# Second mixture, first expert: the next expert's weights prepared nine steps sooner, and the Sinkhorn rounds in rising order

## The chip, the core and the metric

The kernel runs on one core of a Trainium2 chip. The metric is device time in microseconds of one execution; lower is better. The core has TensorE (PE: matmuls and transposes, into PSUM), VectorE (DVE), ScalarE (ACT), GpSimd (POOL) and SyncE (SP, whose queue issues most loads). Each engine works off its own instructions strictly in their order and waits on semaphores for the others.

## The reference

Three stages in one program: attention with queries averaged in pairs, a first mixture that dispatches each token to one expert, and a second mixture in which all 8 experts work on all 1152 tokens. Only the second is touched. Its inputs are x (1152 x 512), w1 (8 x 512 x 1024) and w2 (8 x 1024 x 512):

```python
logits = x @ w_gate
logits = logits - logits.max()
P = np.exp(logits)
for _ in range(8):
    P /= P.sum(1, keepdims=True) + 1e-09
    P /= P.sum(0, keepdims=True) + 1e-09
    P *= N / E
for e in range(E):
    h = np.maximum(x @ w1[e], 0.0)
    ye = h @ w2[e]
    out += P[:, e:e + 1] * ye
```

## The kernel before

Every fp32 operand is split into a pair of fp16 matrices, a high and a low part, scaled by a power of two that comes from its largest magnitude. For a weight matrix that takes: four size reductions on DVE, one per quarter (`amx`, tile `wmx`); a transpose on PE that brings the 128 lanes together (`fa`, tile `wmt`); a small matmul that spreads the result (`fb`, tile `wmp`); a few instructions of DVE to the scale; then high parts on ACT (L159) and low parts on DVE (L164).

In the second mixture the first expert (`e == 0`, weights number 8) runs a plain first layer: 24 steps of 12 matmuls, over three chunks of 256, 384 and 512 columns of tokens with 8 steps each (tile `g`; ACT writes `hh`, DVE writes `hl`). Then the second layer: 9 tiles of tokens with 24 matmuls each (L1550 to L1552), each folded into `acc` by DVE. From the second expert on, layer 1 is one level of Winograd's form (L1373), so its w1 needs four sums on POOL (`w1_sums`, L1341 and L1344) between its parts `o1` to `o7`, and x needs sums too: `x_sums`, eight sums on POOL for each half of the tokens with splits on ACT and DVE, done once, while the first expert runs.

The order of all this beside the matmuls is written out by hand in slots. `at(sl, k, f)` puts a piece of work into slot k, `run(sl, k)` emits it behind step k. For the first expert slots 0 to 23 are the steps of layer 1, and slots 24 to 41 (NL is 24) are two for each tile of layer 2: one in its middle, one at its end. `PM` holds the slots of the weights' work, `XS` those of the rest. The raw w1 and then the raw w2 of the next expert use one buffer (`r`), so the load of w2 waits until all of w1 has been worked off, and the load of the following w1 until all of w2 has been.

The gate's eight Sinkhorn rounds stand in layer 1 as well. A round is `sk_col` (a column sum by a matmul, tile `pc`, L1262, and four instructions of DVE) and `sk_row` (four of DVE). The eighth is `sk_end` in place of a row step: it writes the gate `Pf`, from which `fac` and so `acc` follow. `XS[20]` to `XS[27]` are the slots of the eight rounds; before, the last two are 23 and 22.

Of the kernel before, what the change touches and what calls it, by code (L numbers as in the profile page):

```python
# [42 lines left out]
AHX_ENG = ['dve', 'dve', 'dve', 'act', 'act', 'any', 'act', 'any', 'dve']  # L43
LAG = 6
LOD = 1
PM = [21, 22, 22, 24, 26, 27, 27, 33, 0, 8, 4, 4, 4, 6, 7, 9, 10, 10, 13, 13, 9, 13, 16, 15, 18, 20, 0, 6, 13]
BGP = 100
XM = "ddddddppp"
# [2 lines left out]
LT = 3  # L51
LE = 4
XTA = [1, 3, 5, 7]
XS = [0, 1, 1, 2, 5, 5, 6, 7, 0, 0, 3, 3, 5, 6, 7, 8, 9, 9.5, 10, 11, 12, 13.5, 15, 16, 18, 20, 23, 22]
LG = [3, 2, 2, 2]
PT = {6: 'act'}
A_SCALE = 2.0 ** A_BITS
# [4 lines left out]
def attn_moe_sinkhorn(ctx, tc, q, k, v, wg1, wa1, wa2, wg2, wb1, wb2, out, cap):  # L62
# [21 lines left out]
    wZ = ctx.enter_context(tc.tile_pool(name="wZ", bufs=1))  # L84
    drp = ctx.enter_context(tc.tile_pool(name="drp", bufs=1, space=DRAM))

# [1 line left out]
    idf = cst.tile([P, P], F32, name="idf")  # L88
    make_identity(nc, idf)
    idh = cst.tile([P, P], F16, name="idh")  # L90
# [26 lines left out]
        nc.sync.dma_start(wg1f, wg1.rearrange("(c p) e -> p c e", p=P))  # L117
        nc.sync.dma_start(wg2f, wg2.rearrange("(c p) e -> p c e", p=P))

# [1 line left out]
    def pow2(pool, m, n, T, tag):  # L121
        b = pool.tile([P, n], I32, tag=tag + "b", name=tag + "b")
        s = pool.tile([P, n], I32, tag=tag + "s", name=tag + "s")
# [39 lines left out]
    def lo(o, i, s, h):  # L163
        nc.vector.scalar_tensor_tensor(out=o, in0=i, scalar=s, in1=h, op0=ALU.mult, op1=ALU.subtract)  # L164

# [1 line left out]
    wraw = {}  # L167
    wset = {}
    WN = ("1h", "1l", "2h", "2l", "s")
# [98 lines left out]
    xd = drp.tile([N, 2 * DM], F16, name="xd")  # L268
    yd = drp.tile([E * cap, DM], F32, name="yd")

    # ================= attention =================
    rt = ctx.enter_context(tc.tile_pool(name="rt", bufs=1))
    lgs = rt.tile([P, NT, E], F32, name="lgs")
    mrow = rt.tile([P, NT], F32, name="mrow")
# [624 lines left out]
            if t >= ji:  # L899
                tl_av(t)  # L900

    # ================= routing =================
    actx.close()
    wpools[0, 1] = ctx.enter_context(tc.tile_pool(name="wB2", bufs=1))
    m1 = ExitStack()
# [77 lines left out]
    fac1 = rt.tile([P, NT], F32, name="fac1")  # L983
    tt(fac1, gate, isx, ALU.mult)

    # ================= first mixture: dispatched experts =================
    gp = m1.enter_context(tc.tile_pool(name="gp", bufs=2))
    xTs = {}
    wgh = rt.tile([P, KD, E], F16, name="wgh")
# [21 lines left out]
    def at(slots, k, f):  # L1011
        slots.setdefault(k, []).append(f)
# [34 lines left out]
                    at(slots, base + l[j][c], lambda j=j, c=c: lo_(j, c))  # L1047

    def keep_warm(n):
        # the array's clock halves after a few idle microseconds  # L1050
        pw = ps_i.tile([P, 512], F32, tag="mi", name="warm")
        for _ in range(n):
            nc.tensor.matmul(pw[:, :cap], lhsT=idh, rhs=iocap, start=True, stop=True)
# [100 lines left out]
    keep_warm(80)  # L1154
    sg, ig = yq["g"]

    # ================= combine =================
    m1.close()
    m2 = ctx.enter_context(tc.tile_pool(name="m2", bufs=1))
    m2s = ctx.enter_context(tc.tile_pool(name="m2s", bufs=2))  # L1160
# [74 lines left out]
            out=lg2[:, t, :], in0=pl[:, :E], scalar1=isx2[:, t : t + 1], scalar2=None, op0=ALU.mult  # L1235
        )

    # ================= Sinkhorn gate, run beside the first expert =================
    Pm = m2.tile([P, NT, E], F32, name="Pm")
    Pf = m2.tile([P, NT, E], F32, name="Pf")  # L1240
    rs = m2.tile([P, NT], F32, name="rs")
# [32 lines left out]
        nc.vector.tensor_scalar(out=rs, in0=isx2, scalar1=sg, scalar2=None, op0=ALU.mult)  # L1274
        tt(Pf, Pm, bc(rs), ALU.mult)

    # ================= second mixture: every expert on every token =================
    # From its second expert on, the first layer is one level of Winograd's form of
    # Strassen's product, on halves of w1's columns, of the model width and of the tokens.
    wx = []  # L1280

    def wino_open():
# [176 lines left out]
    for e in range(E):  # L1459
        i = E + e  # L1460
        sl = {}
        for k_, fs_ in carry.items():
            for f_ in fs_:
                at(sl, k_, f_)
        carry = {}
        if e == 0:
            for t in range(2):
                c_max(t)
            c_scale(0, 2)
            for f_ in (c_hi, c_lo, c_tr):  # L1470
                for t in (1, 0):
                    f_(t)
            for t in range(2, 5):
                c_max(t)
            c_scale(2, 5)
            for t in range(2, 5):
                at(sl, XS[t - 2], lambda t=t: (c_hi(t), c_lo(t)))
                at(sl, XS[t - 2] + 1, lambda t=t: c_tr(t))
            for t in range(5, NT):
                at(sl, XS[3], lambda t=t: c_max(t))  # L1480
            at(sl, XS[3], lambda: c_scale(5, NT))
            for t in range(5, NT):
                at(sl, XS[t - 1], lambda t=t: (c_hi(t), c_lo(t)))
                at(sl, XS[t - 1] + 1, lambda t=t: c_tr(t))
            for t in range(NT):
                at(sl, XS[8 + t], lambda t=t: c_lg(t))
            at(sl, XS[17], lambda: red(nmx, lg2.rearrange("p t e -> p (t e)"), ALU.max))
            at(sl, XS[18], sk_a)
            at(sl, XS[19], sk_b)
            at(sl, XS[19], sk_row)  # L1490
            at(sl, XS[19], wino_open)
            for k_ in range(8):
                at(sl, XS[20 + k_], sk_col)
                at(sl, XS[20 + k_], sk_row if k_ < 7 else sk_end)
            w1_plan(sl, i + 1, PM[:4], PM[4:6], PM[6])
            for s_ in range(2):
                xs_ = x_sums(s_)
                for j in range(9):
                    at(sl, NL + PM[8 + s_] + j, lambda xs_=xs_: next(xs_))
            b_ = PM[7]  # L1500
        elif e + 1 < E:
            w1_plan(sl, i + 1, PM[20:24], PM[24:26], NL + PM[26])
            b_ = NL + PM[27]
        if e + 1 < E:
            at(sl, b_, lambda i=i: w_load(i + 1, 1))
            amx, fa, fb, hi_, lo_ = [lambda *a_, i=i, m=m: preps[i + 1][m](*a_) for m in range(5)]
            w2q = [lambda c=c, amx=amx: amx(1, c) for c in range(4)]
            w2q += [lambda fa=fa: fa(1), lambda fb=fb: fb(1)]
            w2q += [lambda c=c, hi_=hi_, lo_=lo_: (hi_(1, c), lo_(1, c)) for c in range(4)]
            nxt = {}  # L1510
            if e + 2 < E:
                w2q.append(lambda i=i: w_load(i + 2, 0))
            for g_, k_ in zip(w2q, PM[10:20] + [PM[28]]):
                if b_ + k_ < NL + 18:
                    at(sl, b_ + k_, g_)
                else:
                    nxt.setdefault(b_ + k_ - NL - 18, []).append(g_)
        if e == 0:
            w1h, w1l = [wset[i][n_] for n_ in WN[:2]]
            for ch in range(3):  # L1520
                cs_ = slice(XG[ch] * P, (XG + [NT])[ch + 1] * P)
                QC = cs_.stop - cs_.start
                for f in range(KF):
                    fs = slice(f * P, (f + 1) * P)
                    ps = ps_g.tile([P, 512], F32, tag="g", name="g3")
                    for c in range(KD):
                        nc.tensor.matmul(ps[:, :QC], lhsT=w1h[:, c, fs], rhs=xT2[:, c, cs_], start=(c == 0), stop=False)
                        nc.tensor.matmul(
                            ps[:, :QC], lhsT=w1h[:, c, fs], rhs=xT2[:, KD + c, cs_], start=False, stop=False
                        )  # L1530
                    run(sl, ch * KF + f - 0.5)
                    for c in range(KD):
                        nc.tensor.matmul(
                            ps[:, :QC], lhsT=w1l[:, c, fs], rhs=xT2[:, c, cs_], start=False, stop=(c == KD - 1)
                        )
                    nc.scalar.activation(hh[:, f, cs_], ps[:, :QC], AF.Relu)
                    nc.vector.scalar_tensor_tensor(
                        out=hl[:, f, cs_], in0=ps[:, :QC], scalar=0.0, in1=hh[:, f, cs_], op0=ALU.max, op1=ALU.subtract
                    )
                    run(sl, ch * KF + f)  # L1540
        else:
            rest = wino_l1(i, sl)
        w2h, w2l, i12 = [wset[i][n_] for n_ in WN[2:]]
        fac = m2s.tile([P, NT], F32, tag="fac", name=f"fac{e}")
        nc.vector.tensor_scalar(out=fac, in0=Pf[:, :, e], scalar1=i12, scalar2=None, op0=ALU.mult)
        for k_, t in enumerate((0, 1, 5, 2, 3, 4, 6, 7, 8) if e else range(NT)):
            ts_ = slice(t * P, (t + 1) * P)
            ps = ps_g.tile([P, 512], F32, tag="g", name="g4")
            for f in range(KF):
                nc.tensor.matmul(ps[:, :DM], lhsT=hh[:, f, ts_], rhs=w2h[:, f], start=(f == 0), stop=False)  # L1550
                nc.tensor.matmul(ps[:, :DM], lhsT=hh[:, f, ts_], rhs=w2l[:, f], start=False, stop=False)  # L1551
                nc.tensor.matmul(ps[:, :DM], lhsT=hl[:, f, ts_], rhs=w2h[:, f], start=False, stop=(f == KF - 1))  # L1552
                if f == 3 and (k_ or not e):
                    run(sl, NL + 2 * k_)
            if e and not k_:
                rest()
                run(sl, NL)
            if e == 0:
                nc.vector.tensor_scalar(
                    out=acc[:, t, :], in0=ps[:, :DM], scalar1=fac[:, t : t + 1], scalar2=None, op0=ALU.mult  # L1560
                )
            else:
                nc.vector.scalar_tensor_tensor(  # L1563
                    out=acc[:, t, :], in0=ps[:, :DM], scalar=fac[:, t : t + 1], in1=acc[:, t, :],
                    op0=ALU.mult, op1=ALU.add,
                )
            if e == E - 1:
                nc.sync.dma_start(out[t * P : (t + 1) * P, :], acc[:, t, :])
            run(sl, NL + 2 * k_ + 1)
        assert not sl, sorted(sl)  # L1570
        carry = nxt if e + 1 < E else {}
# [29 lines left out]
```

## Time and profile before

| what | value |
|---|---|
| device time, median of 3 runs | 1335.86 us (1335.6 to 1338.24) |
| span of the profiled execution | 1332.0 us |
| PE busy | 1211.0 us, 91% |
| DVE busy | 985.2 us, 74% |
| ACT busy | 610.5 us, 46% |
| POOL busy | 362.4 us, 27% |

The page gives no device time of its own for the profiled execution; its span runs from the first to the last instruction, 3.9 us less than the median. Busy time of PE counts slow matmuls as busy, so the granted clock has to be read beside it. The second mixture fills about the last 770 us of the span; its first expert runs from 566.6 to 690.7 us.

### The profile page before, as it was taken

To read this page: it belongs to the slowest core of one execution; us is meant where nothing else is said; L and a number is where in the kernel's file an instruction comes from. 1 tells how busy PE (TensorE), PEld (TensorE's weight loads), DVE (VectorE), ACT (ScalarE), POOL (GpSimd) and SP (SyncE) were. 2 spreads that over 40 slices of the span, in tenths; PEclk is the share of its full clock that TensorE was granted. 3 is DMA by queue.
4 is the path that set the end of the run, shared out by engine and by line. 5 is a ranking of instruction groups with operands and counts; after the bars stand their busy time and mean duration, and the time that the engine had idled before them with its cause. 6 is when DMAs were issued, how large, how long until landed. Compare 5 with 4: busy or idle time off the path is not lost.

```text
span 1332.0 us, 21634 instructions
## 1 busy us (share of the span) xinstructions
PE 1211.0 (91%) x8796; PEld 771.6 (58%) x8796; DVE 985.2 (74%) x1752; ACT 610.5 (46%) x974; POOL 362.4 (27%) x193
## 2 busy tenths in 40 slices
PE   5786879786999999799879999999999999999998
PEld 2444545454777777674346466466475574664763
DVE  5989989997776768467869668677587595686741
ACT  5777767764778876341223323234133133232320
POOL 2665757672124321202631100101011011001000
PEclk9878888886999999999989999999999999999999
DMA  7999999994797784200011110110110211101001
GB/s 219 210 209 227 210 209 206 195 178 128 243 287 237 232 226 162 86 5 1 1 63 64 59 69 1 64 64 1 63 64 1 80 48 62 66 1 63 1 20 53
DMA packets 232996, 145.82 MB, mean 109 GB/s; under 512 B 188672, under 2 KB 197888, under 8 KB 232896
## 3 DMA queue, kind: packets, MB, share of 16 engines
q1 hardware_dynamic: 228560, 133.16, 40.0%
q0 software_dynamic: 2256, 7.08, 1.7%
q10 hardware_dynamic: 2080, 4.19, 0.9%
q8 instruction: 69, 1.13, 0.3%
q14 instruction: 31, 0.25, 0.1%
HBM read 88.38 MB, written 9.44 MB: 73 GB/s over the span
## 4 chain that ended last, share of the span: by engine, by line
PE 58%; DVE 22%; DMA 7%; ACT 6%; issue 4%; POOL 1%; SPq 1%; another core or an unknown queue 0%; POOLq 0%; ACTq 0%; DVEq 0%
PE g L1550 7%; PE g L1552 7%; PE g L1551 7%; PE ba L1373 6%; PE b L1373 4%; PE bb L1373 4%; DVE wmx L135 4%; DMA r<-in_moe_w_dram 3%; PE ps L478 3%; DVE hl L1388 3%; PE g L1139 2%; DVE a L494 2%; PE g L1141 2%; PE g L1140 2%; DMA aT<-ahl 2%
## 5 line engine op out<-in xcount | busy, mean ns | idle before, releaser
L1373 PEld LDWEIGHTS <-o 128*128 128x128 f16 x2352 | 229.3, 98 | 72.6 <-issue 12.2
L515 POOL TENSOR_TENSOR ahl<-a,ahl 128x1152 f16<-128x1152 f32 x71 | 173.3, 2450 | 89.4 <-DVE ahl L460 47.3
L1386 ACT ACTIVATE hh<-wt 128x288 f16<-128x288 f32 x168 | 74.4, 443 | 218.6 <-DVE wt L1396 218.6
L1373 PE MATMUL ba<-T,o 128*128 128x288 f16 x1008 | 150.9, 286 | 4.0 <-DVE wt L1396 3.9
L478 PE MATMUL ps<-kT,qT 128*128 128x384 f16 (+3 forms) x480 | 123.0, 395 | 26.3 <-DVE a L494 25.9
L135 DVE TENSOR_REDUCE wmx<-r 128x1 f32<-128x1024 f32 x96 | 113.9, 1208 | 30.7 <-DMA r<-in_moe_w_dram 30.6
L1396 DVE TENSOR_TENSOR wt<-ba,wt 128x288 f32<-128x288 f32 x168 | 74.2, 453 | 58.9 <-PE ba L1373 44.4
L1563 DVE SCALAR_TENSOR_TENSOR acc<-g,fac,acc 128x512 f32<-128x512 f32 x63 | 47.1, 748 | 95.5 <-PE g L1552 95.3
L1552 PE MATMUL g<-w2h,hl 128*128 128x512 f16 x288 | 110.9, 385 | 0.0
L1551 PE MATMUL g<-w2l,hh 128*128 128x512 f16 x288 | 110.8, 385 | 0.0
L1550 PE MATMUL g<-w2h,hh 128*128 128x512 f16 x288 | 110.7, 384 | 0.0
L1550 PE MATMUL g<-w,hh 128*128 128x512 f16 x288 | 109.2, 379 | 0.0
L1551 PE MATMUL g<-w,hh 128*128 128x512 f16 x288 | 109.2, 379 | 0.0
L1552 PE MATMUL g<-w,hl 128*128 128x512 f16 x288 | 109.2, 379 | 0.0
L494 DVE TENSOR_SCALAR_CACHE_REDUCE a<-ps,nsc 128x1152 f32<-128x1152 f32 x72 | 101.1, 1406 | 9.2 <-PE ps L478 7.4
L1373 PE MATMUL bb<-xT,o 128*128 128x288 f16 x672 | 100.6, 286 | 4.2 <-DVE wt L1396 4.0
L1373 PE MATMUL b<-xT,o 128*128 128x288 f16 x672 | 100.7, 286 | 0.0
L1388 DVE SCALAR_TENSOR_TENSOR hl<-wt,hh 128x288 f16<-128x288 f32 x168 | 94.4, 563 | 7.8
L1552 PEld LDWEIGHTS <-hl 128*128 128x128 f16 x576 | 56.7, 98 | 68.9 <-issue 1.6
L1551 PEld LDWEIGHTS <-hh 128*128 128x128 f16 x576 | 56.7, 98 | 65.7 <-issue 1.4
L1550 PEld LDWEIGHTS <-hh 128*128 128x128 f16 x576 | 56.6, 98 | 65.6 <-issue 1.3
L500 ACT ACTIVATE a<-a,nm 128x1152 f32<-128x1152 f32 x72 | 89.7, 1252 | 1.9
(331 smaller groups left out, 2533.9 us busy)
## 6 DMA issues: line engine op xcount, KB each, us to landing
r<-in_moe_w_dram SPq DMA_DIRECT2D x27, 2048.0 KB, 8.8
r<-in_moe_w_dram SPq DMA_DIRECT2D x12, 512.0 KB, 4.5
kf<-in_k_dram SPq DMA_DIRECT2D x8, 576.0 KB, 4.6
vf<-in_v_dram SPq DMA_DIRECT2D x8, 576.0 KB, 4.6
qf<-in_q_dram SPq DMA_DIRECT2D x16, 256.0 KB, 3.3
r<-in_moe_w_dram ACTq DMA_DIRECT2D x2, 2048.0 KB, 10.7
yd<-ysb SPq DMA_DIRECT2D x16, 256.0 KB, 8.8
xd<-xhl SPq DMA_DIRECT2D x9, 256.0 KB, 2.3
```

Source lines behind the costliest of these rows:

```text
L135: nc.vector.tensor_reduce(out=o, in_=i, axis=[AX.X, AX.XY, AX.XYZ][len(i.shape) - 2], op=ALU.max, apply_absolute_value=True)
L478: nc.tensor.matmul(ps[lo_:hi_, j, :CW], lhsT=qT[i][: P - i * D, t, lo_:hi_], rhs=kT[b][: P - i * D, 3 * j : 3 * j + 3, :], start=(i == 0), ...
L494: nc.vector.tensor_scalar(out=a, in0=ps[:, :, :CW], scalar1=nsc, scalar2=3.0e38, op0=ALU.mult, op1=ALU.min, accum_out=m)
L500: nc.scalar.activation(a, a, AF.Exp, bias=nm, scale=-1.0)
L515: eng.tensor_tensor(out=ahl[:, 1], in0=af, in1=ahl[:, 0], op=ALU.subtract)
L1373: nc.tensor.matmul(ps[:, :TC], lhsT=o[:, oi, c, fs], rhs=x_[:, xi, c, ss], start=start and n == 0, stop=n == len(mms) - 1, skip_group_chec ...
L1386: nc.scalar.activation(hh[o], c, AF.Relu)
L1388: lambda: nc.vector.scalar_tensor_tensor(out=hl[o], in0=c, scalar=0.0, in1=hh[o], op0=ALU.max, op1=ALU.subtract)
L1396: nc.vector.tensor_tensor(out=o, in0=ps[:, :TC], in1=b, op=ALU.add)
L1550: nc.tensor.matmul(ps[:, :DM], lhsT=hh[:, f, ts_], rhs=w2h[:, f], start=(f == 0), stop=False)
L1551: nc.tensor.matmul(ps[:, :DM], lhsT=hh[:, f, ts_], rhs=w2l[:, f], start=False, stop=False)
L1552: nc.tensor.matmul(ps[:, :DM], lhsT=hl[:, f, ts_], rhs=w2h[:, f], start=False, stop=(f == KF - 1))
```

## The change

A new table `E0` gives the first expert's weight work slots of its own. The four reductions of the next w1 go from slots 21, 22, 22, 24 to 9, 10, 12, 14, `fa` and `fb` from 26 and 27 to 16 and 17, and the eight steps of high parts, low parts and POOL sums from slot 27 on to slot 18 on. The two sets of sums of x keep slots 24 and 32. The load of w2 goes from slot 33 to 27, the rest of w2's work from slots 37 and later to 30 to 40, and the load of the following w1 from the fifth slot of the next expert to slot 41. The slots of the Sinkhorn rounds go from 12, 13.5, 15, 16, 18, 20, 23, 22 to 12, 13.5, 15, 17, 18, 20, 21, 23. Comments are taken out, too.

```diff
+E0 = dict(am=[9, 10, 12, 14], f=[16, 17], s=18, xs=[24, 32], ld=27, q=[30, 31, 32, 33, 35, 36, 37, 38, 39, 40, 41])
 PM = [21, 22, 22, 24, 26, 27, 27, 33, 0, 8, 4, 4, 4, 6, 7, 9, 10, 10, 13, 13, 9, 13, 16, 15, 18, 20, 0, 6, 13]
...
-XS = [0, 1, 1, 2, 5, 5, 6, 7, 0, 0, 3, 3, 5, 6, 7, 8, 9, 9.5, 10, 11, 12, 13.5, 15, 16, 18, 20, 23, 22]
+XS = [0, 1, 1, 2, 5, 5, 6, 7, 0, 0, 3, 3, 5, 6, 7, 8, 9, 9.5, 10, 11, 12, 13.5, 15, 17, 18, 20, 21, 23]
...
-            w1_plan(sl, i + 1, PM[:4], PM[4:6], PM[6])
+            w1_plan(sl, i + 1, E0["am"], E0["f"], E0["s"])
             for s_ in range(2):
                 xs_ = x_sums(s_)
                 for j in range(9):
-                    at(sl, NL + PM[8 + s_] + j, lambda xs_=xs_: next(xs_))
-            b_ = PM[7]
+                    at(sl, E0["xs"][s_] + j, lambda xs_=xs_: next(xs_))
+            b_ = E0["ld"]
...
-            for g_, k_ in zip(w2q, PM[10:20] + [PM[28]]):
+            for g_, k_ in zip(w2q, PM[10:20] + [PM[28]] if e else [k_ - b_ for k_ in E0["q"]]):
```

The rows of the changed kernel below have line numbers that are higher by one, since a line was added above them.

On PE, before, the transpose `wmt` of the next w1 stood in the middle of the second tile of layer 2 (`hh` and `hl` are the hidden values, `w2h` and `w2l` the parts of the first expert's w2, `g_7946` that tile's result):

```order
L1551 MATMUL g_7946<-w2l_6781,hh 128x512
L1552 LDWEIGHTS hl
L1552 MATMUL g_7946<-w2h_6780,hl 128x512
L144 MATMUL wmt<-idf,wmx_9_7861 4x128
L1550 LDWEIGHTS hh
L1550 MATMUL g_7946<-w2h_6780,hh 128x512
```

In the changed kernel it stands in layer 1, between step 16 (`g_7746`) and step 17 (`g_7767`), whose operands are the parts of the first expert's w1 and the turned x, `xT`:

```order
L1534 MATMUL g_7746<-xT_7115,w1l_6922 128x512
L145 MATMUL wmt<-idf,wmx_9_7601 4x128
L1528 LDWEIGHTS w1h_6921
L1528 MATMUL g_7767<-xT_7115,w1h_6921 128x512
L1529 LDWEIGHTS w1h_6921
```

The transpose moved from layer 2 into layer 1.

On POOL, before, the sums of x (`xsa`, `xsb`) and those on the next w1 (`s` and the raw weights `r`) were mixed, at the start of layer 2:

```order
L1300 TENSOR_TENSOR xsa_7929<-xT_7115 128x576 x2
L1300 TENSOR_TENSOR xsb_7930<-xsa_7929 128x576
L1341 TENSOR_TENSOR s_9_7995<-r_6679 128x1024
L1300 TENSOR_TENSOR xsa_7929<-xT_7115 128x576
L1344 TENSOR_TENSOR r_6679<-r_6679 128x2x512
L1300 TENSOR_TENSOR xsa_7929<-xsa_7929 128x576
```

In the changed kernel the four sums on w1 come first, and behind them the sums of x:

```order
L1342 TENSOR_TENSOR s_9_7833<-r_6679 128x1024
L1345 TENSOR_TENSOR r_6679<-r_6679 128x2x512
L1345 TENSOR_TENSOR r_6679<-s_9_7833,r_6679 128x2x512
L1345 TENSOR_TENSOR r_6679<-r_6679 128x2x512
L1301 TENSOR_TENSOR xsa_7972<-xT_7115 128x576 x2
L1301 TENSOR_TENSOR xsb_7973<-xsa_7972 128x576
```

The sums on w1 no longer stand behind the sums of x, which wait for the end of layer 1.

On DVE, before, the end of layer 1 held reductions and Sinkhorn steps between the low parts of the hidden values, `hl` (here those of steps 21 and 22; L916 to L919 and L1266 to L1274 are Sinkhorn, `Pf` the gate):

```order
L1537 SCALAR_TENSOR_TENSOR hl<-g_7846,hh 128x512
L135 TENSOR_REDUCE wmx_9_7861<-r_6679 128x1
L1537 SCALAR_TENSOR_TENSOR hl<-g_7863,hh 128x512
L916 TENSOR_REDUCE cs<-pc 128x8
L1266 TENSOR_SCALAR cs<-cs 128x8
L1267 RECIPROCAL cs<-cs 128x8
L1268 SCALAR_TENSOR_TENSOR Pm<-Pm,cs 128x72
L1274 TENSOR_SCALAR rs<-isx_7117,wgss 128x9
L919 TENSOR_TENSOR Pf<-Pm,rs 128x72
L135 TENSOR_REDUCE wmx_9_7861<-r_6679 128x1 x2
```

In the changed kernel, from the same step 21 on:

```order
L165 SCALAR_TENSOR_TENSOR o_9_7831<-r_6679,w0s,o_9_7831 128x1024
L1538 SCALAR_TENSOR_TENSOR hl<-g_7881,hh 128x512
L917 TENSOR_REDUCE cs<-pc 128x8
L1267 TENSOR_SCALAR cs<-cs 128x8
L1268 RECIPROCAL cs<-cs 128x8
L1269 SCALAR_TENSOR_TENSOR Pm<-Pm,cs 128x72
L917 TENSOR_REDUCE rs<-Pm 128x9
L1257 TENSOR_SCALAR rs<-rs 128x9
L1258 RECIPROCAL rs<-rs 128x9
L920 TENSOR_TENSOR Pm<-Pm,rs 128x72
L165 SCALAR_TENSOR_TENSOR o_9_7850<-r_6679,w0s,o_9_7850 128x1024
```

Where reductions stood there are now low parts of the next w1 (`o_9`), ahead of and between the last Sinkhorn rounds, and the gate is written two steps later.

## Rows read from the trace of the kernel before

**Rows 1.** Waits of PE, 566.6 to 735 us: total us, times, longest.

```profile
PE wmt L144 <- DVE wmx L135: 12.3, 3, 8.0
...
PE pc L1262 <- DVE Pm L919: 0.6, 2, 0.3
```

**Rows 2.** Timeline of PE: start, duration, what, idle before and who ended it.

```profile
626.22 0.38 PE L1550 MATMUL g<-w2h,hh 128*128 128x512 f16 x1
...
638.25 0.27 PE L144 MATMUL wmt<-idf,wmx 128*4 128x128 f32 x1 [4.10 <-DVE wmx L135]
...
684.83 0.37 PE L144 MATMUL wmt<-idf,wmx 128*4 128x128 f32 x1 [7.99 <-DVE wmx L135]
...
690.71 0.91 PE L1373 MATMUL b<-xT,o 128*128 128x288 f16 x6
```

**Rows 3.** Windows: PE, PEld, DVE, ACT, POOL busy, granted clock, DMA.

```profile
638.30:643.00 4.70, 4.70 (x16) 1.83 (x16) 1.17 (x4) 0.00 (x0) 0.00 (x0) 0.64 0.00 0
643.00:676.80 33.80, 33.80 (x157) 15.20 (x156) 28.42 (x24) 11.91 (x14) 26.59 (x13) 1.00 0.14 51
...
684.90:690.70 5.80, 5.80 (x15) 2.14 (x15) 1.28 (x4) 0.00 (x0) 0.00 (x0) 0.51 0.00 0
```

**Rows 4.** Timeline of DVE in layer 2 of the first expert.

```profile
628.08 2.33 DVE L135 TENSOR_REDUCE wmx<-r 128x1 f32<-128x1024 f32 x2
...
633.49 1.94 DVE L1256 TENSOR_SCALAR rs<-rs 128x9 f32<-128x9 f32 x1
...
647.63 1.28 DVE L164 SCALAR_TENSOR_TENSOR o<-r,w0s,o 128x1024 f16<-128x1024 f32 x1
```

**Rows 5.** Timelines of POOL and of ACT.

```profile
633.06 2.34 POOL L1344 TENSOR_TENSOR r<-r 128x1024 f32<-128x1024 f32 x1
...
708.45 2.36 POOL L1341 TENSOR_TENSOR s<-r 128x1024 f32<-128x1024 f32 x1 [31.52 <-DMA r<-in_moe_w_dram]
...
644.17 2.19 ACT L159 ACTIVATE o<-r,w0s 128x1024 f16<-128x1024 f32 x2 [17.33 <-DVE w0i L131]
```

**Rows 6.** Timeline of DVE: first, sixth and last row of a Sinkhorn round.

```profile
608.08 0.22 DVE L916 TENSOR_REDUCE cs<-pc 128x8 f32<-128x72 f32 x1
...
609.31 0.17 DVE L1256 TENSOR_SCALAR rs<-rs 128x9 f32<-128x9 f32 x1
...
609.76 0.23 DVE L919 TENSOR_TENSOR Pm<-Pm,rs 128x72 f32<-128x72 f32 x1
```

**Rows 7.** The chain that ended last: start, duration, what.

```profile
666.39 4.19 DVE o L164 x2
670.64 8.18 DMA r<-in_moe_w_dram
678.85 3.47 DVE wmx L135 x3
```

**Rows 8.** Timelines of DVE and of PE in the next expert's first layer.

```profile
698.32 2.48 DVE L164 SCALAR_TENSOR_TENSOR w<-r,w1s,w 128x1024 f16<-128x1024 f32 x2 [0.59 <-ACT w L159]
...
701.22 0.90 PE L1373 MATMUL ba<-T,o 128*128 128x288 f16 x6 [0.78 <-DVE wt L1396]
...
703.29 0.90 PE L1373 MATMUL ba<-T,o 128*128 128x288 f16 x6 [0.44 <-DVE wt L1396]
...
719.02 0.90 PE L1373 MATMUL bb<-xT,o 128*128 128x288 f16 x6 [0.87 <-DVE wt L1396]
```

**Rows 9.** Timeline of DVE and PE in layer 1 of the first expert.

```profile
591.93 0.23 DVE L916 TENSOR_REDUCE nmx<-lg 128x1 f32<-128x72 f32 x1
...
592.74 0.27 PE L144 MATMUL gmxt<-idf,nmx 128*1 128x128 f32 x1
...
607.14 0.41 PE L1262 MATMUL pc<-Pm,onf 128*128 128x72 f32 x2 [0.34 <-DVE Pm L919]
```

**Rows 10.** Windows: steps 10 to 15, and steps 16 to 23.

```profile
590.50:604.00 13.50, 13.25 (x94) 8.23 (x93) 8.21 (x31) 3.30 (x7) 0.00 (x0) 1.00 0.00 1
604.00:626.20 22.20, 21.86 (x109) 10.66 (x108) 14.20 (x46) 4.67 (x8) 0.63 (x1) 1.00 0.00 0
```

## The prediction

> **What bounds the kernel now.** TensorE (PE) is busy 91% of the span (the table above), so time is won where PE stands still or runs slowly. I first read the waits of PE from the start of the second mixture's first expert to the end of the next expert's first layer [rows 1]: one pair stands out, the transpose `wmt` waiting for `wmx`, the size reductions of the next expert's weights, 12.3 us in three waits. The timeline of PE gives the places [rows 2]: layer 2 of the first expert begins at 626.22; `wmt` for w1 waits 4.10 us and runs at 638.25; `wmt` for w2 waits 7.99 us and runs at 684.83; the next expert starts at 690.71. Last, the windows of that layer [rows 3]: behind each wait the granted clock is low, 0.64 over a stretch of 4.7 us and 0.51, the 1.2 GHz level, over one of 5.8 us, while in the long stretch between it is 1.00 (2.4 GHz) and 157 matmuls take 33.8 us, 0.215 us each.
>
> Why is each `wmx` late? The first set queues on VectorE (DVE) behind Sinkhorn work that runs beside GpSimd (POOL): an instruction on 9 elements a lane takes 1.94 us and ends at 635.43 [rows 4], just as POOL's sum, begun at 633.06, ends at 635.40 [rows 5]; with POOL idle a whole column-and-row round of eight such instructions takes from 608.08 to 609.99, 1.9 us [rows 6]. The second set is the last link of a chain [rows 7]: the low parts of w1 end at 670.6, only then can the buffer take the load of w2 (8.18 us), then come the reductions, then `wmt`.
>
> **The change, part by part.**
>
> *Layer 2 of the first expert.* It has 9 x 24 matmuls x 0.215 = 46.5 us and keeps one small pair, `wmt` and `wmp` of w2, about 0.3 us: 46.8, against 690.71 - 626.22 = 64.5 us now. So 17.7 us can go: 4.1 + 8.0 of waiting, the rest low clock and w1's pair, which moves. I take all of it, and name the cover. `wmt` of w1 now stands behind step 16 of layer 1; its four reductions are emitted at steps 9, 10, 12 and 14 (they wait for no load, as before [rows 4]) and end by the count below near 606.4, step 16 near 607.8. For w2: layer 2 starts near 629.2; DVE then has the last low parts, the Sinkhorn end and `acc`, beside POOL's sums of x, and ends the last low part near 643.7; the load gives 652; four reductions of 1.2 us, with `acc` and a split of x between them, give 659; `wmt`, behind the sixth tile, stands at 629.2 + 6 x 5.2 = 660.3. The cover is 1.3 us, and each further us is paid.
>
> *Start of the next expert.* The high and low parts of w2 leave its first products, where DVE spends 2.48 us on two of them at 698.32, and PE waits 0.78 and then 0.44 us [rows 8]. Gain 1.2. In layer 2 they lie beside matmuls that don't need them. The load of w1 for the second next expert is issued earlier too, with nothing ahead of it on SP's queue; POOL's first sum on it (2.36 us) therefore comes earlier than at 708.45 [rows 5]. There the next wait of PE is 0.87 us at 719.02 [rows 8], so I price this at nothing, at most one such wait.
>
> *Layer 1 of the first expert,* which takes the work. DVE is idle for 5.3 us in steps 10 to 15 and 8.0 us in steps 16 to 23 [rows 10]. In come: three more reductions (3.6; the fourth was there), the way to the scales, seven small instructions at 0.2 us [rows 6], 1.4, and four low parts at 1.28 us [rows 4], 5.1. ScalarE (ACT) gets high parts at 1.1 us each [rows 5], and has room. POOL's four sums on w1, 2.34 us each [rows 5], now run here. All this reaches PE because each Sinkhorn column sum, `pc`, is a matmul in PE's order and waits for DVE. I shifted the old timeline step by step:
> - step 10: a reduction stands ahead of `nmx`, which ended at 592.16, about 0.45 us sooner than `gmxt` at 592.74 needs it [rows 9]. With 1.2 us more, PE waits 0.7.
> - step 12: POOL's second sum starts behind the second reduction, near 595.7, and holds a Sinkhorn instruction until 598.0; `pc` waits 0.7 more.
> - step 18: five small instructions to the scale stand ahead of `pc`'s operand; it waits 0.35.
> - step 21: a low part (1.3) and POOL's third sum (0.75 of it) lengthen the round before; `pc` waits 1.35. POOL's fourth sum falls into the round after, but the next `pc` stands two steps on and just finds it done.
> - w1's `wmt` and `wmp`: 0.3. The `pc` behind step 16 moves to 17, and its wait of 0.34 [rows 9] goes.
>
> Sum 0.7 + 0.7 + 0.35 + 1.35 + 0.3 - 0.34 = 3.05. The bounds: only the pair's 0.3, if idle DVE time takes the rest; and from above all that comes in, 3.6 + 1.4 + 5.1, a Sinkhorn round of 1.9 that moves ahead, POOL's 4 x 2.34 = 9.4, and 0.3: 21.7. I stay near the lower end, because 13.3 us of idle time lie in these steps.
>
> [...] The rows agree with the holding (the 1.94 us above ends within 0.03 us of POOL's sum), and reductions beside POOL stay at 1.2 us [rows 4]. At its worst, each of the four sums holding DVE for its full length on the path, layer 1 would lose 9.4 us to POOL where I charge 1.45, and the time would be 1328.
>
> *The Sinkhorn rounds.* Before, a last row and column step ran after the gate had been taken, unused; now all eight rounds count. The instructions are the same. The gate comes later, near 639, and the first `acc` with it; results rotate through six PSUM banks, so PE would wait only for an `acc` some five tiles, 26 us, late.
>
> **Sum.** -17.7 - 1.2 + 3.05 = -15.85. The profiled span is 1332.0 us, 3.9 below the median of the runs; I assume that the part around the span stays. 1335.86 - 15.85 = 1320.0.
>
> **The rivals.**
> - *Layer 1 takes it for nothing.* -17.7 - 1.2 + 0.3 = -18.6: 1317.3. For it: more idle DVE time than work, apart from POOL's holding. Against: the work stands right ahead of `nmx` and `pc`, not in the idle time.
> - *The wait for w2 moves instead of going.* Each us by which the last low part ends after 645 is a wait behind the sixth tile. At 650 that is 5 us, and the low clock behind it adds 2 to 3, as behind the old waits [rows 3]: 1327.5. For it: two low parts beside POOL took 4.19 us [rows 7], and POOL now has eight sums of x in a row here. Against: before, w1's sums were mixed with them, and those are done by now.
> - *DVE becomes the bound of layer 1, slower than before.* Place: steps 9 to 23, where PE stops at each `pc` for a queue with 21.7 us more in it. If idle time takes none of it, the loss exceeds the gains of 18.9: 1338.7. It decides the sign from 18.9 us on. Against: 13.3 us of idle time would have to stay idle.
> - *It does nothing.* If the waits hung on something else than order, say a late load of w1, they would stay: 1335.9. Against: the reductions waited for no load, and both transposes stand elsewhere now.
>
> **How the numbers follow.** Forecast 0.63, its own range 1317 to 1325; layer 1 for nothing 0.14; w2's wait moved 0.15; DVE the bound 0.04; nothing 0.04. A measurement of this kernel tells about 0.2%, 2.7 us, from no change. The first three are faster, 0.92; same 0.04; slower 0.04. The range goes from below the free case to past the moved wait: 1314.5 to 1329.
>
> **What would show it.** Right: no `wmt` wait above 1 us, a granted clock of 1.00 through layer 2 and some 47 us for it; layer 2 begins about 3 us later than at 626.22; new waits of PE at `gmxt` and `pc` of 3 us in all, the longest at step 21; the load of w2 issued near 644; the next expert without its first two waits. Wrong: `pc` waits of many us with DVE held by POOL; a `wmt` wait behind the sixth tile; waits of the next expert's first products for a DVE that POOL's early sum holds.

## The result, and the profile after

The changed kernel takes 1320.78 us (median of 4 runs, 1318.97 to 1321.45) against 1337.05 us of the kernel before (4 runs, 1335.6 to 1339.05): ratio 0.9877 [0.9863, 0.9891], 16.3 us less. Beside the last experiments both ran once more: 1317.46 against 1333.42 us, 0.9877 [0.986, 0.9893]. The forecast was 1320.0, with 1314.5 to 1329 as its range. The profiled span is 1318.9 us (before 1332.0). Line numbers in the changed kernel are one higher.

The waits of PE from 566.6 to 722 us answer to [rows 1] (total us, times, longest):

```profile
...
PE pc L1263 <- DVE Pm L920: 3.0, 3, 1.4
PE wmp L155 <- DVE wmd L149: 1.1, 1, 1.1
PE ba L1374 <- DVE wt L1397: 0.4, 1, 0.4
PE gmxt L145 <- DVE nmx L917: 0.3, 1, 0.3
...
PE wmt L145 <- DVE wmx L136: 0.2, 1, 0.2
```

The 12.3 us of `wmt` are down to 0.2 (that one stands in the next expert); `pc` rose from 0.6 to 3.0, and `wmp` has a wait of 1.1 that was not there (the line left out at the top is the wait for x at the stage's start, ahead of every edit). The timeline of PE gives the places [rows 2, 8, 9]:

```profile
592.98 0.27 PE L145 MATMUL gmxt<-idf,nmx 128*1 128x128 f32 x1 [0.31 <-DVE nmx L917]
...
598.42 0.44 PE L1263 MATMUL pc<-Pm,onf 128*128 128x72 f32 x2 [0.86 <-DVE Pm L920]
...
623.42 0.41 PE L1263 MATMUL pc<-Pm,onf 128*128 128x72 f32 x2 [1.37 <-DVE Pm L920]
...
629.74 0.41 PE L1263 MATMUL pc<-Pm,onf 128*128 128x72 f32 x2 [0.73 <-DVE Pm L920]
...
661.07 0.27 PE L145 MATMUL wmt<-idf,wmx 128*4 128x128 f32 x1
665.04 0.35 PE L155 MATMUL wmp<-wmd,onf 4*128 4x4 f32 x2 [1.11 <-DVE wmd L149]
```

The first four are steps 10, 12, 21 and 23 of layer 1; `wmt` of w2 runs at 661.07 without a wait. The window of layer 2 [rows 3] has the clock at 1.00 throughout:

```profile
629.90:677.00 47.10, 45.99 (x216) 20.94 (x216) 37.39 (x46) 11.26 (x14) 22.73 (x15) 1.00 0.14 45
```

To compare runs I cut PE's timeline at the first matmuls of step 8, of layer 2, of the next expert and of what follows its first layer (us; Sum adds the first three columns). Steps 0 to 7 are left out of Sum: at the stage's start, ahead of every edit, the clock of 5 us was 0.50 to 1.00 from run to run, and these steps took 18.0 to 19.6 us accordingly. The stage of the expectations below has them, and stands in a column of its own.

| kernel | steps 8 to 23 | layer 2 | next expert's first layer | Sum | stage with steps 0 to 7 | ratio to before, same chip |
|---|---|---|---|---|---|---|
| before | 40.59 | 64.49 | 44.05 | 149.13 | 168.11 | 1 |
| changed | 44.60 | 48.29 | 42.16 | 135.05 | 153.44 | 0.9877 [0.9863, 0.9891] |
| changed, again | 44.58 | 48.27 | 42.16 | 135.01 | 154.44 | 0.9877 [0.986, 0.9893] |
| e1_rounds | 41.63 | 61.24 | 44.48 | 147.35 | 166.92 | 1.0009 [0.9996, 1.0022] |
| e2_w1_only | 44.58 | 47.13 | 44.02 | 135.73 | 154.12 | 0.9913 [0.9895, 0.993] |
| e3_old_rounds | 46.07 | 47.68 | 42.02 | 135.77 | 153.79 | 0.9901 [0.9871, 0.9932] |
| e4_warm | 40.58 | 60.09 | 43.92 | 144.59 | 163.90 | 0.9983 [0.9967, 0.9999] |
| e5_s22 | 42.84 | 56.07 | 41.88 | 140.79 | 160.18 | 0.9931 [0.9912, 0.995] |
| e6_no_sums | 42.29 | 47.24 | 42.17 | 131.70 | 151.17 | 0.9883 [0.9863, 0.9902] |
| e7_combo | 43.73 | 47.15 | 42.14 | 133.02 | 152.22 | 0.9879 [0.9858, 0.99] |
| e9_early_am | 41.68 | 58.41 | 43.98 | 144.07 | 163.48 | 0.9965 [0.9951, 0.9978] |
| e11_am8 | 43.57 | 48.05 | 42.18 | 133.80 | 153.12 | 0.9879 [0.986, 0.9899] |
| e10_combo2 | 42.35 | 47.15 | 42.28 | 131.78 | 151.15 | 0.9861 [0.9845, 0.9877] |

The two profiles of the changed kernel agree within 0.02 us in each part, so a difference of some tenths can be read in this table, where device times scatter by 2 to 8 us. Device times of different sets can't be set side by side: the kernel before ran again with each set, and its median was 1337.05 us in the first, 1330.02 beside e1 to e4, 1334.77 beside e5, e6, e7 and e9, and 1333.42 beside e10, e11 and the repeat. Beside e1 to e4 the gains by device time are 0.8 to 3.3 us smaller than by Sum, whose row of before comes from the first set; why before was faster there stays open. The change: +4.0 - 16.2 - 1.9 = -14.1 in the stage. The spans differ by 13.1 us: steps 0 to 7 took 0.6 less, the stage began 0.35 later, and all behind it took 1.2 longer.

### The profile page after: what moved, and what is told of

It reads as the page before. It is cut to its first block, busy times and chain, and to the rows that moved or that the text cites. A ratio compares the mean times of both kernels' runs of the same rounds, so it can differ in the third digit from the quotient of the medians.

```text
span 1318.9 us, 21631 instructions
## 1 busy us (share of the span) xinstructions
PE 1199.8 (91%) x8796; PEld 766.9 (58%) x8796; DVE 980.4 (74%) x1752; ACT 610.2 (46%) x974; POOL 356.8 (27%) x193
## 4 chain that ended last, share of the span: by engine, by line
PE 59%; DVE 20%; DMA 8%; ACT 5%; issue 5%; POOL 2%; SPq 1%; another core or an unknown queue 0%; POOLq 0%; DVEq 0%; ACTq 0%
PE g L1551 7%; PE g L1553 7%; PE g L1552 7%; PE ba L1374 7%; PE b L1374 4%; PE bb L1374 4%; DVE wmx L136 4%; DMA r<-in_moe_w_dram 4%; DVE hl L1389 3%; PE ps L479 2%; PE g L1140 2%; DVE a L495 2%; PE g L1142 2%; PE g L1141 2%; PE g L1103 2%
## 5 line engine op out<-in xcount | busy, mean ns | idle before, releaser
L479 PE MATMUL ps<-kT,qT 128*128 128x384 f16 (+3 forms) x480 | 118.2, 382 | 28.3 <-DVE a L495 27.8
L551 PE MATMUL po<-vs,aT 128*128 128x130 f16 (+1 forms) x720 | 80.1, 237 | 15.5 <-DMA aT<-ahl 9.5
```

Of the source, the lines that this page charges most:

```text
L479: nc.tensor.matmul(ps[lo_:hi_, j, :CW], lhsT=qT[i][: P - i * D, t, lo_:hi_], rhs=kT[b][: P - i * D, 3 * j : 3 * j + 3, :], start=(i == 0), ...
L551: nc.tensor.matmul(pof[lo_:hi_, :], lhsT=aT[:, c, lo_:hi_], rhs=vs[:, b, c, :], start=(c == 0), stop=False,)
```

## The experiments

**e1_rounds**: the kernel before, with the order of the Sinkhorn rounds alone.

```diff
-XS = [..., 13.5, 15, 16, 18, 20, 23, 22]
+XS = [..., 13.5, 15, 17, 18, 20, 21, 23]
```

> The kernel before with only the Sinkhorn rounds in rising order. My theory (the transposes wmt wait for a late DVE queue, twice, and each wait has its own cause): the unused round of 5.8 us leaves the queue ahead of the last reduction of w1, so the first wait of 4.1 us and the low clock behind it go, the second wait of 8.0 us stays, because the load of w2 still waits for late low parts: about 6 us faster than before, 1330 to 1332. Rival (the order of the rounds is the whole gain): near 1321, no wait of wmt above 1 us.

Measured: 1331.42 against 1330.02 us, no change; layer 2 is only 3.3 us shorter and layer 1 1.0 longer (Sum 1.8 less): the theory missed. The first `wmt` waits 2.54 us where I expected none, the second 8.45 (timeline of PE):

```profile
635.75 0.27 PE L144 MATMUL wmt<-idf,wmx 128*4 128x128 f32 x1 [2.54 <-DVE wmx L135]
...
681.14 0.37 PE L144 MATMUL wmt<-idf,wmx 128*4 128x128 f32 x1 [8.45 <-DVE wmx L135]
```

The timelines of DVE and, behind it, of POOL say why:

```profile
627.49 1.21 DVE L1268 SCALAR_TENSOR_TENSOR Pm<-Pm,cs 128x72 f32<-128x72 f32 x1
628.62 2.32 DVE L1274 TENSOR_SCALAR rs<-isx,wgss 128x9 f32<-128x9 f32 x1
630.98 1.26 DVE L919 TENSOR_TENSOR Pf<-Pm,rs 128x72 f32<-128x72 f32 x1
632.27 2.21 DVE L1545 TENSOR_SCALAR fac<-Pf,i 128x9 f32<-128x9 f32 x1
634.40 1.21 DVE L135 TENSOR_REDUCE wmx<-r 128x1 f32<-128x1024 f32 x1
```

```profile
627.22 1.40 POOL L1300 TENSOR_TENSOR xsb<-xsa 128x576 f32<-128x576 f32 x1
628.57 2.35 POOL L1341 TENSOR_TENSOR s<-r 128x1024 f32<-128x1024 f32 x1
630.88 1.27 POOL L1300 TENSOR_TENSOR xsa<-xT 128x576 f32<-128x576 f16 x1
632.11 2.35 POOL L1344 TENSOR_TENSOR r<-r 128x1024 f32<-128x1024 f32 x1
```

Each of four small instructions ends within 0.1 us of an instruction of POOL: 628.70 and 628.62, 630.94 and 630.92, 632.24 and 632.15, 634.48 and 634.46. While POOL's queue is full, DVE gets one of these four done for each instruction of POOL, though they have only 9 to 72 elements a lane; the last reduction stands behind four. A round there instead of another only changes which small instructions pay. The Trainium skill, "SBUF — State Buffer", section "Who interferes with whom", has DVE and POOL take a shared port pair as a lock for a whole instruction; it counts `tensor_scalar` among the forms that can take it and, where POOL's instruction reads SBUF, any form with two inputs in SBUF. The four here are of these kinds, and the rows agree with it, down to 9 elements a lane.

**e2_w1_only**: the changed kernel, with the load and the work of w2 as late as before; the part on w1 is left.

```diff
-E0 = dict(..., ld=27, q=[30, 31, 32, 33, 35, 36, 37, 38, 39, 40, 41])
+E0 = dict(..., ld=33, q=[37, 37, 37, 39, 40, 42, 43, 43, 46, 46, 46])
```

> The changed kernel with the work on w2 (load, reductions, scale, high and low parts) put back into its old slots; only w1 is early. Theory: the second wait hung on late low parts of w1, so it does not come back, the load of w2 is again issued near 645 although it is written later; the high and low parts of w2 lie at the start of the next expert again and cost PE 1 to 2 us there: 1320.5 to 1322.5. Rival (the early slots of w2 remove the second wait): the wait of several us comes back, 1327 or more.

Measured: 1319.29 against 1330.02 us, layer 2 at 47.13, no `wmt` wait in it; the waits at the start of the next expert are back, as in [rows 8] (timeline of PE):

```profile
690.90 0.90 PE L1374 MATMUL ba<-T,o 128*128 128x288 f16 x6 [0.78 <-DVE wt L1397]
...
692.97 0.90 PE L1374 MATMUL ba<-T,o 128*128 128x288 f16 x6 [0.44 <-DVE wt L1397]
```

The waits are as the theory said, and the load of w2 is again issued right behind the last low part of w1. The time is not: 1320.5 to 1322.5 was meant against a before of 1337, and the 10.7 us gained here are fewer than the changed kernel's 16; the intervals of the ratios don't touch. Sum finds 0.7 us of this, and behind the stage e2's profile is as long as that of before (597.8 and 597.2), so the rest stays open, as for the other runs of this set (above). By the stage, w1 ahead of layer 2 brings the whole gain there; w2's own part of the edit brings 1.9 us in the next expert and costs layer 2 the wait of `wmp`, 1.1.

**e3_old_rounds**: the changed kernel, with the rounds in their old order.

```diff
-XS = [..., 13.5, 15, 17, 18, 20, 21, 23]
+XS = [..., 13.5, 15, 16, 18, 20, 23, 22]
```

> The changed kernel with the rounds in the old order (16, 18, 20, 23, 22 at the end). Theory: the unused round stands beside POOL's sums of x and delays the last low part of w1 by 3 to 5 us, more than the cover of the load of w2, so wmt or wmp of w2 waits 2 to 5 us: 1322 to 1327. Rival (the order of the rounds is the whole gain): back to 1333 or more. Second rival (no matter): 1320.8.

Measured: 1317.41 against 1330.02 us, Sum 135.77, that is 0.7 above the changed kernel, none of it told by device time. The theory missed: no `wmt` waits, and the second rival was right. PE waits 3.26 us, but for a `pc` at the end of layer 1, and `wmp` waits less:

```profile
629.95 0.41 PE L1263 MATMUL pc<-Pm,onf 128*128 128x72 f32 x2 [3.26 <-DVE rs L1275]
661.28 0.27 PE L145 MATMUL wmt<-idf,wmx 128*4 128x128 f32 x1
664.64 0.35 PE L155 MATMUL wmp<-wmd,onf 4*128 4x4 f32 x2 [0.50 <-DVE wmd L149]
```

With e1 this settles that the rising order is not the cause of the gain: alone it takes 1.8 us off Sum, and beside the rest of the change 0.7.

**e4_warm**: the kernel before, with 30 and 62 matmuls into an unused bank ahead of the two transposes; all waits of DVE stay, PE is only kept running.

```diff
+            at(sl, 26, lambda: keep_warm(30))
...
+            at(sl, 40, lambda: keep_warm(62))
```

> The kernel before with matmuls on constants (30 and 62 of 288 columns, 3.6 and 7.4 us) ahead of the two transposes, so that PE works through most of both waits. It measures the low clock by itself. Theory: the stretches behind the waits, 4.7 and 5.8 us at 0.64 and 0.51, return to 1.00 and give back 4 to 5 us; the two waits shrink to under 1 us each as counted, but the time to the transposes stays: 1332 to 1333. Rival (the slow stretches do not come from PE's standing still): no change, 1336 to 1337.

Measured: 1328.82 against 1330.02 us, ratio 0.9983; layer 2 falls by 4.4 us. The first transpose is no sooner, 12.05 us behind the start of layer 2 (12.03 before). The second comes 56.99 behind it instead of 58.61: `wmp` of w1, in PE's order behind the first transpose, runs 1.5 sooner at the full clock, and with it w1's scale and the chain to w2. The window behind the first transpose has a clock of 1.00 (0.64 in [rows 3]):

```profile
634.70:639.70 5.00, 5.00 (x25) 2.29 (x25) 2.19 (x9) 0.71 (x1) 0.00 (x0) 1.00 0.00 0
```

So of the 16.2 us that layer 2 gained, about 4.4 are the clock behind the waits, with what it brings forward, and the waits the rest.

**e5_s22**: the changed kernel, with the parts and sums of w1 four steps later, and the load of w2 three slots later.

```diff
-E0 = dict(..., s=18, xs=[24, 32], ld=27, q=[30, 31, ...])
+E0 = dict(..., s=22, xs=[24, 32], ld=30, q=[30, 31, ...])
```

> The changed kernel with the parts and sums of w1 four steps later (slots 22 to 29 instead of 18 to 25), the load of w2 at slot 30. By stage, from the first matmul of layer 1 to the next expert's second layer: before 168.1 us, changed 153.4. Theory (the load of w2 waits for the last low part of w1, and the cover was 1 to 2 us): layer 1 is 1 to 2 us shorter, the last low part ends 7 to 10 us later, and wmt of w2 waits about that much with a low clock behind it: stage 159 to 164. Rival (the early place of the work on w2 is enough): 153 or less, no wait above 1 us.

Measured: 1324.29 against 1334.77 us; layer 2 at 56.07, `wmt` of w2 waits 6.81. The timelines of DVE and PE show the chain of [rows 7] again, low part, load, reduction, `wmt`:

```profile
646.57 1.76 DVE L165 SCALAR_TENSOR_TENSOR o<-r,w0s,o 128x1024 f16<-128x1024 f32 x1
656.59 1.22 DVE L136 TENSOR_REDUCE wmx<-r 128x1 f32<-128x1024 f32 x1 [4.63 <-DMA r<-in_moe_w_dram]
...
663.32 0.37 PE L145 MATMUL wmt<-idf,wmx 128*4 128x128 f32 x1 [6.81 <-DVE wmx L136]
```

The last low part ends at 648.33, 23.1 us behind the start of layer 2 (625.27); in the changed kernel it is 14.9 (644.92 and 629.99), so 8.1 later, within the 7 to 10 expected. There the cover, from the end of the last reduction to `wmt` in PE's order, is 0.8 us, and from low part to first reduction it takes 0.5 less here (8.3 against 8.8): 8.1 - 0.8 - 0.5 = 6.8, the wait. So this end sets the second wait, and what passes the cover is paid, with the low clock behind it (0.61 over 5 us).

**e6_no_sums**: the changed kernel, but POOL's four sums on the next w1 are left out (the parts take the raw quarters in their place, so that expert's result is another).

```diff
-            nc.gpsimd.tensor_tensor(out=st["s1"], in0=a21, in1=a22, op=ALU.add)
+            if i != E + 1:
+                nc.gpsimd.tensor_tensor(out=st["s1"], in0=a21, in1=a22, op=ALU.add)
...
+            if i == E + 1:
+                return lambda: None
...
-        s1_ = lambda: st["s1"]
+        s1_ = (lambda: a22) if i == E + 1 else (lambda: st["s1"])
```

> The changed kernel without POOL's four sums on the next w1 (left out, for this one expert: its parts are taken from the unsummed weights). Theory (POOL holds Sinkhorn instructions in steps 12, 20 and 21 and PE pays): the waits of pc fall from 0.86, 1.37 and 0.73 to about 0.3, 0.6 and 0; layer 1 takes 61 instead of 63.0 us, stage near 151.3. Rival (the mere number of DVE instructions sets layer 1): layer 1 stays at 63.

Measured: steps 8 to 23 at 42.29, 2.3 us of the 4.0 gone. The instruction that ran 0.78 us beside POOL in the changed kernel (597.06, row below) takes 0.17 here, the waits at steps 12 and 21 fall to 0.25 and 0.58 (timelines of DVE and PE), and that at step 23 is gone, as the theory had it:

```profile
596.66 0.17 DVE L1257 TENSOR_SCALAR rs<-rs 128x9 f32<-128x9 f32 x1
```

```profile
597.40 0.44 PE L1263 MATMUL pc<-Pm,onf 128*128 128x72 f32 x2 [0.25 <-DVE Pm L920]
...
621.68 0.41 PE L1263 MATMUL pc<-Pm,onf 128*128 128x72 f32 x2 [0.58 <-DVE Pm L920]
```

**e7_combo**: the changed kernel, with the last rounds one step apart, so that they end before POOL's third and fourth sums, the parts and sums of w1 two steps later, and the load and work of w2 one slot later.

```diff
-E0 = dict(..., s=18, xs=[24, 32], ld=27, q=[30, 31, 32, 33, 35, ...])
+E0 = dict(..., s=20, xs=[24, 32], ld=28, q=[31, 32, 33, 34, 36, ...])
-XS = [..., 13.5, 15, 17, 18, 20, 21, 23]
+XS = [..., 13.5, 15, 16, 17, 18, 19, 20]
```

> A version to beat the changed kernel: Sinkhorn rounds one a step at 15 to 20, the parts and sums of w1 two steps later (20 to 27), so that POOL's later sums meet no Sinkhorn round; the load and work of w2 one slot later. Theory (holding by POOL is most of the price of layer 1): waits of pc of 1 to 2 us in all, no wait at wmp; stage 151 to 153. Rival (DVE work as such): a round a step is more than DVE does in 2.6 us, waits of 3 us or more, stage 154 or more.

Measured: 1318.68 against 1334.77 us; Sum 133.02, 2.0 below the changed kernel, and no wait of `wmp`. `pc` still waits 0.86 at step 12 and 0.66 at step 16. Its device time doesn't tell it from the changed kernel.

**e9_early_am**: the kernel before, with only the four reductions of w1 early; the transposes stay where they were.

```diff
-            w1_plan(sl, i + 1, PM[:4], PM[4:6], PM[6])
+            w1_plan(sl, i + 1, [9, 10, 12, 14], PM[4:6], PM[6])
```

> The kernel before with one thing changed: the four reductions of w1 at steps 9, 10, 12, 14. The rounds keep their old order. After the miss with the rounds alone, the theory is that any small DVE instruction that needs the port stands in POOL's way there, so what counts is that the reductions no longer stand behind such instructions: no wait at the first wmt, the clock behind it 1.00, the second wait stays near 8 us: stage 168.1 - 6 + 1 (a wait more of gmxt and pc) = 163. Rival (the first wait has another cause): the wait stays above 2 us.

Measured: 1329.8 us, Sum 144.07, layer 2 at 58.41, as expected. The wait of `wmt` is gone with nothing but this. A smaller one comes behind it at `wmp`, since held Sinkhorn instructions still stand ahead of the steps between the two on DVE; the second `wmt` still waits 7.71 (timeline of PE):

```profile
634.44 0.27 PE L144 MATMUL wmt<-idf,wmx 128*4 128x128 f32 x1
638.67 0.35 PE L154 MATMUL wmp<-wmd,onf 4*128 4x4 f32 x2 [1.37 <-DVE wmd L148]
```

This settles what e1 left open: the first wait of `wmt` was the reductions' place behind held Sinkhorn work.

**e11_am8** and **e10_combo2**: the changed kernel and e7, each with the reductions one or two steps earlier, two of them at step 8; **after_again** is the changed kernel beside them on the same chip.

```diff
-E0 = dict(am=[9, 10, 12, 14], ...)
+E0 = dict(am=[8, 8, 10, 12], ...)
```

> The changed kernel with the reductions of w1 alone moved one or two steps earlier (steps 8, 8, 10, 12). Theory: the waits at gmxt and at pc of step 12 fall from 1.2 us together to 0.3, the waits of steps 21, 23 and at w2's column maxima (1.4, 0.7, 1.1) stay, steps 8 to 23 take about 43.6 us and the stage about 152.4. Rival: the waits keep their sum, steps 8 to 23 at 44.6, the stage 153.4.

> The changed kernel with the sums of x at step 20, w2's first transposes at 28 with their queue one step later, the Sinkhorn rounds 13 to 20 one step apart, and all four reductions of w1 one or two steps earlier (two in step 8, where VectorE stands idle ahead of a high part). Theory (what the first layer still pays is GpSimd's starts falling on VectorE's small instructions): GpSimd's second sum then runs beside reductions and high parts, the waits at gmxt (0.3) and at pc of step 12 (0.86) go, steps 8 to 23 take about 42.2 us against 44.6 of the changed kernel and 43.7 of the seventh run, and the stage about 150.7. Rival (the starts only fall on other small instructions): the same sum of waits at other places, steps 8 to 23 at 43.5 to 45, the stage 152 to 153.5.

> The changed kernel itself, once more beside the two, for a direct comparison. Both theories: steps 8 to 23 at 44.6 us, layer 2 at 48.3, the stage at 153.4 to 154.4 as its first microseconds have a clock of 0.7 or of 0.5, and a ratio of 0.986 to 0.989.

What was expected of e10 misnames two things: what stands at step 20 (`s`) are the parts and sums of w1, not the sums of x, and what stands at 28 (`ld`) is the load of w2. The rounds are those of e7.

Measured: 1318.32, 1315.11 and 1317.46 us, against 1333.42 of before. In both variants the wait at `gmxt` goes and that at step 12 falls from 0.86 to 0.25, in e11 as the theory had it; steps 8 to 23 take 43.57 and 42.35 (expected 43.6 and 42.2), Sum 133.80 and 131.78 against 135.01. The stage of e11, 153.12, is 0.7 over the theory's, because steps 0 to 7 took 19.3 us in it and 18.4 in the profile from which I had worked that out. The timeline of PE in e10:

```profile
591.00 0.27 PE L145 MATMUL gmxt<-idf,nmx 128*1 128x128 f32 x1
...
595.83 0.44 PE L1263 MATMUL pc<-Pm,onf 128*128 128x72 f32 x2 [0.25 <-DVE Pm L920]
...
605.40 0.41 PE L1263 MATMUL pc<-Pm,onf 128*128 128x72 f32 x2 [0.28 <-DVE Pm L920]
```

And DVE, while POOL's second sum runs there, from 590.22 for 2.35 us:

```profile
590.46 0.22 DVE L1235 TENSOR_SCALAR lg<-pl,isx 128x8 f32<-128x8 f32 x1
590.71 0.23 DVE L917 TENSOR_REDUCE nmx<-lg 128x1 f32<-128x72 f32 x1
591.70 0.56 DVE L1538 SCALAR_TENSOR_TENSOR hl<-g,hh 128x384 f16<-128x384 f32 x1 [0.76 <-ACT hh L1537]
```

None of the three is longer than without POOL (0.22, 0.23 and 0.56 in the kernel before, where POOL stands still): the sum now lies beside instructions that it does not hold (two read PSUM, one is a reduction). e10 is the best version: 2.35 us under the changed kernel in the medians, where the intervals still overlap, 3.2 in Sum.

## Why the prediction was right

*The cause of the first wait* was as stated [rows 4, 5]: reductions behind held Sinkhorn work. e9 moves them alone and the wait of `wmt` is gone; e1 moves the Sinkhorn rounds alone and a wait stays.

*The cause of the second wait* was the chain [rows 7], which e5 brings back. Its forecast held link by link:

| link | predicted | measured |
|---|---|---|
| layer 2 starts | 629.2 | 629.99 |
| last low part of w1 ends | 643.7 | 644.92 |
| first reduction of w2 can start | 652 | 653.71 |
| last reduction ends | 659 | 660.29 |
| `wmt` in PE's order | 660.3 | 661.07, no wait |

```profile
643.65 1.27 DVE L165 SCALAR_TENSOR_TENSOR o<-r,w0s,o 128x1024 f16<-128x1024 f32 x1
...
653.71 1.22 DVE L136 TENSOR_REDUCE wmx<-r 128x1 f32<-128x1024 f32 x1 [5.46 <-DMA r<-in_moe_w_dram]
...
659.08 1.21 DVE L136 TENSOR_REDUCE wmx<-r 128x1 f32<-128x1024 f32 x1
```

The cover came out at 0.8 us where I had 1.3.

*Layer 2* was put at 46.8 us and took 48.29, so the term of -17.7 came out as -16.2. Two parts are missing from it. Without any wait the layer takes 47.15 (e7, e10), 0.35 more than I worked out. And `wmp`, the second link of the pair, waits 1.11: I followed w2 to `wmt` and stopped there. The DVE rows behind `wmt`, and of the Sinkhorn rounds, in the changed kernel:

```profile
597.06 0.78 DVE L1257 TENSOR_SCALAR rs<-rs 128x9 f32<-128x9 f32 x1
...
623.03 0.23 DVE L920 TENSOR_TENSOR Pm<-Pm,rs 128x72 f32<-128x72 f32 x1
...
625.24 1.77 DVE L1267 TENSOR_SCALAR cs<-cs 128x8 f32<-128x8 f32 x1
...
628.28 1.32 DVE L920 TENSOR_TENSOR Pm<-Pm,rs 128x72 f32<-128x72 f32 x1
...
661.94 1.80 DVE L1309 TENSOR_TENSOR T<-xsb,T 128x576 f16<-128x576 f32 x1
...
663.97 0.92 DVE L149 TENSOR_SCALAR wmd<-idf,wmx 4x4 f32<-4x4 f32 x1
```

and POOL beside them:

```profile
595.47 2.35 POOL L1345 TENSOR_TENSOR r<-r 128x1024 f32<-128x1024 f32 x1 [4.88 <-DVE wmx L136]
...
624.64 2.35 POOL L1345 TENSOR_TENSOR r<-r 128x1024 f32<-128x1024 f32 x1 [2.89 <-DVE o L165]
628.23 2.51 POOL L1301 TENSOR_TENSOR xsa<-xT 128x576 f32<-128x576 f16 x2 [1.24 <-PE g L1529]
...
663.09 1.78 POOL L1301 TENSOR_TENSOR xsb<-xT 128x576 f32<-128x576 f16 x1
```

A split of x takes 1.80 where 0.75 is usual, then `wmd`, 4 x 4 elements, runs from 663.97 to 664.89 and ends with POOL's sum (664.87); `wmp` follows at 665.04.

*Layer 1* was put at +3.05 and came to +4.0 (steps 8 to 23). Step by step, waits of PE: step 10 0.31 (0.7 forecast), step 12 0.86, which is 0.6 more than the 0.25 of a run in which POOL doesn't hold (0.7), step 18 0.17 (0.35), step 21 1.37 (1.35). Not foreseen was step 23, 0.73: I looked for POOL's four sums on w1, and it is the first of the sums of x, at 628.23, that holds the last instruction of that round until 629.60. The sum reaches it only because POOL's fourth sum on w1 had held the round's second instruction until 627.01: in e6, which has the sums of x but not that one, step 23 has no wait. My count had the fourth sum's delay just fit. These places, the pair's 0.3 and the 0.34 that went give 0.31 + 0.6 + 0.17 + 1.37 + 0.73 + 0.3 - 0.34 = 3.1. The other 0.9 us lie at the same places: from the start of one step to that of the next PE loses 0.47 at step 10, 0.61 at 12, 0.36 in 16 to 18, 1.61 in 21 and 22, and 0.97 in 23, so behind most waits 0.16 to 0.24 more than the idle time listed. Of the whole 4.0, 2.3 hang on POOL's sums (e6), where I had charged 1.45. The idle time did take most of the work, as the choice near the lower bound had it.

*The next expert* gained 1.9 where I had 1.2; e2 shows both waits [rows 8] returning when w2's work goes back, and with them the third, 0.85 (0.87 at 719.02 before). The rest of the gain is that third wait, 0.23 now. It goes with the load of the following w1, whose earlier place I had put at nothing or a loss: where that load has landed 6 to 8 us behind the expert's start the wait is 0.2, at 11 us (e7, e10) 0.5 and 0.7, at 17 to 18 (before, e1, e2, e4, e9) 0.7 to 1.3. How the one leads to the other isn't worked out. POOL's earlier sum on that w1 does hold two `hl` for 2.98 us at 686.21, and PE pays 0.3 for it: six matmuls take 0.73 to 0.74 there, and 1.03 once (timeline of PE):

```profile
688.57 0.90 PE L1374 MATMUL bb<-xT,o 128*128 128x288 f16 x6
689.60 0.90 PE L1374 MATMUL ba<-T,o 128*128 128x288 f16 x6
...
704.69 0.90 PE L1374 MATMUL bb<-xT,o 128*128 128x288 f16 x6 [0.23 <-DVE wt L1397]
```

*The rivals.* Layer 1 was not free; w2's wait did move in part, from `wmt` to `wmp`, at 1.1 us instead of 5 and more; DVE did not become the bound.

*The sum* was -15.85, against -14.1 in the stage's profiles and -16.3 and -16.0 in the two pairs of medians. I had read 3.9 us between span and median as time around the span. In every run that lists both, that is 1.7 to 1.8 (1320.69 and 1318.9): by that the profiled execution of before, an estimate from its span, ran about 2 us under the first median, and 3.3 under the later. So the closeness of 1320.0 to 1320.78 is in part luck: the stage's -14.1 from 1335.86 would have given 1321.8; which places of the program the 2 us between stage and medians belong to stays open.

## What to carry to other kernels

When a small step is moved ahead of a busy engine, follow its whole chain to the last link that the waiting engine needs, and list what runs on GpSimd over each link: in these traces VectorE's small instructions between tiles in SBUF (`tensor_scalar`, `tensor_tensor`, `scalar_tensor_tensor`) cost what was left of GpSimd's instruction, up to 2.3 us, not their own 0.2. So put GpSimd's work beside reductions and beside reads of PSUM, which kept their length, and keep short chains that TensorE waits for (a scale, a Sinkhorn round) out of its queue. A test that moves only the preparation, and one that moves only its neighbours, tell the cause of such a wait in two runs.

## What the runs showed of the hardware

- An instruction on 8 or 9 elements a lane, or on 4 x 4, is held as a large one is: 1.77 and 0.92 us beside POOL, where the 128x9 form takes 0.17 without it (e6) and the 4 x 4 one 0.22 (before, at 638.99).
- POOL's instructions are longer beside DVE's, too: in the changed kernel POOL's sum `xsb<-xsa` of 128x576 takes 1.41 us at 657.52, beside a reduction, and 2.26 us at 630.82, beside low parts that take 2.31 and 1.82 instead of 1.28.
- Not every wait was followed by a low clock. Behind waits of PE of 1.1 (changed kernel), 2.5 (e1) and 3.3 us (e3) the next 5 us had a granted clock of 1.00; behind 4.1 (before), 6.8 (e5) and 8.4 us (e1) it was 0.64, 0.61 and 0.54 over about as long. From step 8 on the changed kernel's listed waits are 1.4 us at most, and its clock is 1.00 through layer 1, layer 2 and the next expert's first layer.
